# Seven planned durations of an attention and expert kernel set to other values

## Chip, cores and metric

The kernel runs on one core of a Trainium2 chip. The metric is the device time of one execution in microseconds (us). A core has TensorE (PE; its weight loads are PEld), VectorE (DVE), ScalarE (ACT), GpSimd (POOL) and SyncE (SP); here POOL and SP mainly issue DMA transfers.

## What is computed

```python
s_g = scale * np.matmul(q_g, k_all.transpose(0, 1, 3, 2))      # k_all = [k_g, k_l]
out_g = np.matmul(sm(s_g), v_all)
s_ll = np.where(abs(i - j) <= 32, scale * q_l @ k_l.T, -1e9)   # local band
s_lg = scale * np.matmul(q_l, k_g.transpose(0, 1, 3, 2))
out_l = np.matmul(sm(np.concatenate([s_lg, s_ll], axis=-1)), v_all)
x = np.concatenate([out_g, out_l], axis=2)   # 8 batches x (32 + 512) rows, 8 heads x 64
h = x @ w_in                                 # 4352 rows: 512 -> 2048
g = h * np.clip(h + 3.0, 0.0, 6.0) / 6.0
y = g @ w_out                                # 2048 -> 512
```

8 batches, 8 heads of 64, 512 local rows with a window of 32 to each side, 32 global rows; `sm` is the softmax. The attention output, 4352 rows of 512, goes through the two expert products.

## The kernel before

The kernel doesn't write its order of instructions out. It builds a list of operations (`add`), each with an engine or a choice of two (`BOTH`: ScalarE or VectorE), a planned duration in ns, the operations it depends on, a key (its rank), and the ring buffers that it takes and frees. `Plan.lay` then lays all operations in time: it keeps a time at which each engine is free, and again and again takes the operation that can start first, the lower key first among those that can start within 40 ns of each other. Of an operation with two engines it takes the one on which it would end first. A small model of the two transfer queues (`Transfers`) says when a DMA lands. What comes out is one order for each engine; each engine then runs its instructions in that order, and waits on semaphores where a producer isn't done. The planned times themselves are not in the program. `Plan.fill` puts idle matmuls (L1002) where the planned TensorE order leaves gaps before the first use of a certain accumulator, with a bound on the gap's length.

For batch b and step j (128 rows of q) a `local_step` does:
- the scores of 8 heads on TensorE: 8 matmuls against the global keys (L653) and 32 against the bands (L660) in a double accumulator `s`, of which there is one; the first two steps of batch 0 have another form (L646);
- on VectorE per head an addition of the mask with the minimum taken (L672), on ScalarE the exponential with its sum (L683);
- on VectorE per four heads a reciprocal (L693) and a multiplication into `pn` (L697);
- the turn of `pn` into `et`: up to batch 4 on TensorE (L704) with a copy back, from batch 5 on by a DMA transpose of SP (L715);
- the product with the values, `av` (L733; L725 in batch 0), in two accumulators `a`, against strips `st` of the values which SP copies together (L527) from `ve`, and the copy into `xt`, two casts by ScalarE (L295) or VectorE (L297).

For each batch, `global_steps` does the same for its 32 global rows: scores (L771, L776) that take `s` and both accumulators `a`; maxima (L784 to L788); exponentials on ScalarE (L797); sum and reciprocal (L803, L804); scaling to `pg` (L811); the turn to `eg` by TensorE (L825) or, from batch 5 on, by DMA (L819); the product with the values (L838); the copy to `xg` (L846). `place_kg` copies a batch's global keys (L619).

`moe_local` takes a batch once its attention is done: 16 groups of four matmuls with `w_in` (L860; batch 0 in two halves), each followed by a ReLU on ScalarE (L867) and a multiplication on VectorE (L871) out of one of three accumulators `m`; then 16 groups of four with `w_out` (L882), an output copy (L295, L297) and a store by SP (L897). In the order the first products of one batch stand among the attention steps of the next, and the second products after them. `moe_global` does it for all global rows at the end.

GpSimd's queue issues all loads (L411), SP's the strips, the DMA transposes (L573 for q and k from batch 4 on) and the stores.

Of the kernel before, what the change touches and what calls it, by code (L numbers as in the profile page):

```python
# [78 lines left out]
class Plan:  # L79
# [13 lines left out]
    def add(self, eng, dur, emit, deps=(), key=0.0, acq=None, rel=(), dma=None):  # L93

        o = Op(eng, dur, emit, deps, key, acq, rel, 0, dma)
        o.can = {eng: dur} if isinstance(eng, str) else dict(zip(eng, dur))
        o.n = len(self.ops)
        self.ops.append(o)
        for r in rel:
            r.held += 1  # L100
        return o
# [106 lines left out]
def kernel(  # L208
# [17 lines left out]
    S = Sg + Sl  # L226
    dm, dff = moe_w_in.shape
    NP = H // 2
    NJ = Sl // P
# [59 lines left out]
    add = plan.add  # L289
# [3 lines left out]
    def copy(op, out, in_):  # L293
        if op.eng == "ACT":
            nc.scalar.copy(out=out, in_=in_)  # L295
        else:
            nc.vector.tensor_copy(out=out, in_=in_)  # L297

    BOTH = ("ACT", "DVE")
# [103 lines left out]
    qkT, gT, kg, strip, vload = {}, {}, {}, {}, {}  # L403
# [209 lines left out]
    def place_kg(b, key, g_op=None):  # L613
        r, g = b % 2, (b // 2) % 2
        c0 = r * 2 * G + G

        def ev(op):
            for e in range(2):
                nc.vector.tensor_copy(out=kgz[r][e * D:(e + 1) * D, :, e, :],  # L619
                                      in_=gt[g][e * D:(e + 1) * D, :, c0:c0 + G])  # L620
        deps = [g_op or gT[b // 2], prep["clear"]]
        if b >= 2:
            deps += [S_op[b - 2, j] for j in range(NJ)]
        return add("DVE", 260, ev, deps, key=key)

    def local_step(b, j, key):
        r = b % 2
        kept = b == 0 and j < KEEP
# [8 lines left out]
        def pe(op):  # L637
# [17 lines left out]
            for p in range(NP):  # L655
                for u in range(NU):
                    for e in range(2):
# [2 lines left out]
                        nc.tensor.matmul(out=ps[u * UQ:(u + 1) * UQ, e, p * P + G:(p + 1) * P],  # L660
                                         lhsT=qk[r][rows, 0, p, q0:q0 + UQ],
                                         rhs=qk[r][rows, 1, p, q0 - UQ:q0 + 2 * UQ])
        s = add("PE", 1080 if kept else 960, pe, [qkT[b, j], *keyT[b, j], *(keyT[b, 0 if b == j == 0 else min(j + 1, NJ - 1)][:1] if j < NJ - 1 else ()), kg[b] if kept or b else kg0_op[0]], key=key, acq="S")
        S_op[b, j] = s
        first = None
        exs, trs = [], []
# [22 lines left out]
        for a in range(2):  # L689
# [4 lines left out]
            rec = add("DVE", 95, rc, exs[h0:h1] + [pn_op], key=key - 0.1)  # L694
# [43 lines left out]
        else:  # L738
            vs = []
            for a in range(2):  # L740
                vs.append(add("PE", 235, lambda op, a=a: av(op, a), [e_, *strip[b, j], *vs], key=key - 0.4,
                              acq=f"A{a}", rel=[et_op]))
# [4 lines left out]
        def xe(op, a):  # L747
            src = psA[a].rearrange("k (p u e q) -> k p u e q", p=2, u=NU, e=2)
            for e in range(2):
                copy(op, xt[xt_op[b].slot][e * D:(e + 1) * D, 2 * a:2 * a + 2, j * P:(j + 1) * P].rearrange(  # L750
                    "d p (u q) -> d p u q", u=NU), src[e * D:(e + 1) * D, :, :, e, :])
# [2 lines left out]
            copy(op, xt[xt_op[b].slot][:, :, j * P:(j + 1) * P], psA[0].rearrange("k (p q) -> k p q", p=NP))  # L754
        if tight:
            return [add(BOTH, (480, 610), xa, [*vs, xt_op[b]], key=key - 0.5, rel=vs)]
        return [add(BOTH, (780, 680), lambda op, a=a: xe(op, a), [v, xt_op[b]], key=key - 0.5, rel=[v])
                for a, v in enumerate(vs)]

    xt_op, xdone = {}, {}  # L760

    def global_steps(b, key):
        r, g = b % 2, (b // 2) % 2
        g0 = r * 2 * G
        deps = [gT[b // 2]] + [x for j in range(NJ) for x in keyT[b, j]]

        def pe(op):
# [5 lines left out]
            for p in range(NP):  # L773
                for e in range(2):
                    rows = slice(e * D, (e + 1) * D)
                    nc.tensor.matmul(out=psS[op.slot][p * G:(p + 1) * G, e, :], lhsT=gt[g][rows, p, g0:g0 + G],  # L776
                                     rhs=qk[r][rows, 1, p, UQ:UQ + Sl])
        s = add("PE", 750, pe, deps, key=key, acq=("S", "A0", "A1"))
        gS_op[b] = [s]
        so = add("DVE", 0, lambda op: None, [s], key=key, acq="stat")  # L780

        def red(op):
# [3 lines left out]
                nc.vector.tensor_reduce(out=w[:, 0, 2 + e:3 + e], in_=psA[e][:, 0:G], axis=AX, op=ALU.max)  # L786
            nc.vector.tensor_tensor(out=w[:, 0, 4:6], in0=w[:, 0, 0:2], in1=w[:, 0, 2:4], op=ALU.max)
            nc.vector.tensor_scalar(out=w[:, 0, 6:8], in0=w[:, 0, 4:6], scalar1=-scale, scalar2=None, op0=ALU.mult)  # L788
        rd = add("DVE", 1600, red, [so], key=key)
        xs, sgo, evs = [], [], []  # L790
        for e in range(2):
            sgo.append(add("ACT", 0, lambda op: None, [rd], key=key + 0.1 * e, acq="sg"))
# [8 lines left out]
        def rc(op):  # L801
            w = stat[so.slot]
            nc.vector.tensor_tensor(out=w[:, 1, 4:6], in0=w[:, 1, 0:2], in1=w[:, 1, 2:4], op=ALU.add)  # L803
            nc.vector.reciprocal(out=w[:, 2, 0:2], in_=w[:, 1, 4:6])  # L804
        rec = add("DVE", 150, rc, xs, key=key + 0.1)
        eg_op = None
        for e in range(2):
            po = add("DVE", 0, lambda op: None, [rec], key=key + 0.1, acq="pg")
# [32 lines left out]
        v = add("PE", 590, av, evs + [x for i in range(NV) for x in vload[b, i]], key=key, acq="A0", rel=[eg_op])  # L841
        gav[b] = v

        def xe(op):
            for e in range(2):
                nc.vector.tensor_copy(  # L846
                    out=xg[e * D:(e + 1) * D, :, b * G:(b + 1) * G],
                    in_=psA[0][e * D:(e + 1) * D, 0:256].rearrange("d (p e q) -> d p e q", p=NP, e=2)[:, :, e, :])
        return add("DVE", 400, xe, [v], key=key, rel=[v])

# [82 lines left out]
    lqk, lg, keyT, kg0_op = {}, {}, {}, []  # L935
    for b in range(B):
        if b == 0:
            seq = ["q0", "h", "q1", "k", "v0", "v1", "q2", "v2", "q3", "v3", "v4", "i0", "i1", "i2", "i3", "g"]
            for n, what in enumerate(seq):
                k, i, key = what[0], int(what[1:] or 0), -8.0 + 0.05 * n  # L940
# [38 lines left out]
        if b % 2 == 0:  # L979
            if b == 0:  # L980
                kg[0] = turn_g(0, lg[0][:1], lead - 1.5)
                gT[0] = turn_g(0, lg[0], lead + 0.5, [kg[0]])
                if KEEP < NJ:
                    kg0_op.append(place_kg(0, lead - 1.2 if KEEP == 0 else lead + 0.9, kg[0]))
            else:
                gT[b // 2] = turn_g(b, lg[b // 2], lead - 1.5)
        if b:
            kg[b] = place_kg(b, lead - 1.2)
# [7 lines left out]
        for j in range(NJ):  # L996
            xdone[b, j] = local_step(b, j, lead + j)
        xgd[b] = global_steps(b, lead + 3.6)
        moe_local(b, 4.0 * b + 0.5, 4.0)
    moe_global(4.0 * b + 2.5, 1.5)  # L1000
# [39 lines left out]
```

## Time and profile before

| | us |
|---|---|
| median of 3 runs | 345.37 |
| lowest, highest | 341.38, 347.09 |
| the profiled execution | 346.03 |
| its span, first to last instruction | 344.3 |

| engine | busy us | share of the span |
|---|---|---|
| VectorE | 271.3 | 79% |
| ScalarE | 248.7 | 72% |
| GpSimd | 105.6 | 31% |

Lines of a timeline give start and length in us, engine, source line, operation, the tile written and the tiles read, shapes and a count; in square brackets stands the idle time before and what ended it. Lines of groups give busy us in total and mean ns of one instruction. A line of busy time by stretch gives the stretch, its length, then the busy time of PE, PEld, DVE, ACT and POOL with the number of instructions, the granted TensorE clock as a share of full speed, the DMA share, and GB/s.

### The profile page before, as it was taken

To read this page: it belongs to the slowest core of one execution; us is meant where nothing else is said; L and a number is where in the kernel's file an instruction comes from. 1 tells how busy PE (TensorE), PEld (TensorE's weight loads), DVE (VectorE), ACT (ScalarE), POOL (GpSimd) and SP (SyncE) were. 2 spreads that over 40 slices of the span, in tenths; PEclk is the share of its full clock that TensorE was granted. 3 is DMA by queue.
4 is the path that set the end of the run, shared out by engine and by line. 5 is a ranking of instruction groups with operands and counts; after the bars stand their busy time and mean duration, and the time that the engine had idled before them with its cause. 6 is when DMAs were issued, how large, how long until landed. Compare 5 with 4: busy or idle time off the path is not lost.

```text
span 344.3 us, 10201 instructions
## 1 busy us (share of the span) xinstructions
PE 319.0 (93%) x3804; PEld 182.6 (53%) x3804; DVE 271.3 (79%) x1012; ACT 248.7 (72%) x834; POOL 105.6 (31%) x139
## 2 busy tenths in 40 slices
PE   7889878999979889999999999979999999999995
PEld 5768764555445445454545544444444544546642
DVE  5998898789969599969995999679977996576300
ACT  4999997549968578637995888659967997464402
POOL 8735931685377245703810310013000000000000
PEclk9999999999999999999999999999999999999999
DMA  9999999999999999999999697699953413400012
GB/s 158 195 241 163 163 187 240 159 171 190 213 122 202 224 141 159 217 231 148 190 230 194 125 181 197 152 184 155 197 123 94 71 33 91 131 1 2 30 57 98
DMA packets 158322, 52.19 MB, mean 152 GB/s; under 512 B 142656, under 2 KB 150848, under 8 KB 158272
## 3 DMA queue, kind: packets, MB, share of 16 engines
q0 software_dynamic: 106560, 17.05, 70.3%
q1 hardware_dynamic: 51712, 34.48, 45.2%
q8 instruction: 30, 0.49, 0.6%
q14 instruction: 20, 0.16, 0.2%
HBM read 35.19 MB, written 8.91 MB: 128 GB/s over the span
## 4 chain that ended last, share of the span: by engine, by line
PE 42%; DVE 24%; DMA 16%; ACT 8%; SPq 6%; issue 3%; POOL 0%; POOLq 0%; ACTq 0%; DVEq 0%
PE m L882 20%; PE m L860 14%; DMA st<-ve 8%; DVE gs L871 7%; SPq L527 5%; DVE sm L672 5%; DMA ve<-in_v_l_dram 4%; DVE pn L697 4%; ACT sm L683 3%; ACT t L867 3%; DVE xt L297 2%; PE a L733 2%; DMA sm<-in_q_l_dram 1%; ACT sg L797 1%; PE t L704 1%
## 5 line engine op out<-in xcount | busy, mean ns | idle before, releaser
L882 PE MATMUL m<-wout,gs 128*128 128x512 f16 x544 | 129.0, 379 | 1.4 <-DMA wout<-in_moe_w_out_dram 0.7
L860 PE MATMUL m<-xt,win 128*128 128x512 f16 (+1 forms) x576 | 121.6, 355 | 3.8 <-DVE gs L871 3.1
L683 ACT ACTIVATE sm<-sm,stat 128x128 f32<-128x128 f32 x256 | 100.4, 396 | 22.4 <-DVE stat L672 21.9
L871 DVE SCALAR_TENSOR_TENSOR gs<-t,m 128x512 f16<-128x512 f32 x136 | 91.2, 683 | 16.6 <-ACT t L867 15.9
L867 ACT ACTIVATE t<-m 128x512 f32<-128x512 f32 x136 | 79.8, 595 | 16.5 <-PE m L860 15.8
L860 PEld LDWEIGHTS <-win 128*128 128x128 f16 x640 | 60.0, 97 | 55.1 <-issue 7.7
L882 PEld LDWEIGHTS <-gs 128*128 128x128 f16 x544 | 49.9, 98 | 54.1 <-issue 3.7
L672 DVE CUSTOM_DVE_ANT_0 sm<-s,mask 128x128 f32<-128x128 f32 x256 | 61.0, 283 | 3.1 <-PE s L660 2.0
L683 ACT ACTIVATION_READ_ACCUMULATOR sm<-sm,stat 128x1 f32 x256 | 49.4, 193 | 0.0
L697 DVE TENSOR_TENSOR pn<-sm,stat 128x512 f16<-128x512 f32 x64 | 44.0, 688 | 0.9
L411 POOL DMA_DIRECT2D nat<-in_q_l_dram x30 | 26.8, 894 | 37.6 <-DMA qk<-nat 24.0
L295 ACT COPY ot<-m 128x512 f32<-128x512 f32 x28 | 16.4, 586 | 25.9 <-PE m L882 22.2
L411 POOL DMA_DIRECT2D ve<-in_v_l_dram x40 | 32.2, 821 | 7.7 <-PE m L860 4.8
L411 POOL DMA_DIRECT2D nat<-in_k_l_dram x30 | 26.7, 892 | 12.8 <-DMA nat<-in_k_l_dram 4.9
L295 ACT CAST xt<-a 64x256 f16<-64x256 f32 (+1 forms) x63 | 23.7, 376 | 9.6 <-PE a L733 9.1
L733 PEld LDWEIGHTS <-st 128*128 128x128 f16 x448 | 20.1, 98 | 15.3 <-issue 4.8
L733 PE MATMUL a<-et,st 128*128 128x64 f16 x448 | 22.7, 193 | 4.1 <-DMA st<-ve 4.0
L297 DVE CAST xt<-a 64x256 f16<-64x256 f32 (+1 forms) x53 | 22.6, 426 | 4.8 <-PE a L733 3.6
L411 POOL DMA_DIRECT2D ve<-in_v_g_dram x8 | 4.8, 596 | 53.4 <-PE a L838 53.3
L672 DVE DVE_READ_ACCUMULATOR2_ANT stat<- 128x1 f32 x256 | 21.0, 82 | 0.0
L704 PE MATMUL t<-ident,pn 128*128 128x128 f16 x160 | 13.4, 220 | 1.6 <-DVE pn L697 1.6
L693 DVE RECIPROCAL stat<-stat 128x4 f32<-128x4 f32 x64 | 11.1, 173 | 3.8 <-ACT sm L683 3.4
(88 smaller groups left out, 262.4 us busy)
## 6 DMA issues: line engine op xcount, KB each, us to landing
out_dram<-ot SPq DMA_DIRECT2D x32, 256.0 KB, 3.0
st<-ve SPq DMA_DIRECT2D x14, 384.0 KB, 7.7
nat<-in_q_l_dram POOLq DMA_DIRECT2D x30, 128.0 KB, 8.7
nat<-in_k_l_dram POOLq DMA_DIRECT2D x30, 128.0 KB, 8.5
st<-ve SPq DMA_DIRECT2D x7, 512.0 KB, 8.1
st<-ve SPq DMA_DIRECT2D x14, 256.0 KB, 8.7
ve<-in_v_l_dram POOLq DMA_DIRECT2D x24, 128.0 KB, 6.4
st<-ve SPq DMA_DIRECT2D x18, 128.0 KB, 7.1
```

Of the source, the lines that this page charges most:

```text
L295: nc.scalar.copy(out=out, in_=in_)
L297: nc.vector.tensor_copy(out=out, in_=in_)
L411: nc.gpsimd.dma_start(out=dst(op), in_=src)
L527: nc.sync.dma_start(out=dst, in_=src)
L672: nc.vector.tensor_tensor_reduce(out=sm[sm_op.slot][:, h, :], in0=psS[s.slot][:, e, p * P:(p + 1) * P], in1=m, scale=-scale, scalar=3.0e38 ...
L683: nc.scalar.activation(out=sm[sm_op.slot][:, h, :], in_=sm[sm_op.slot][:, h, :], func=EXP, scale=-1.0, bias=stat[stat_op.slot][:, 0, h:h + 1],
L697: (nc.gpsimd if op.eng == "POOL" else nc.vector).tensor_tensor(out=pn[pn_op.slot][:, h0:h1, :], in0=sm[sm_op.slot][:, h0:h1, :], in1=stat[ ...
L733: nc.tensor.matmul(out=psA[a][:, c0:c0 + 64], lhsT=st[r][:, u * NJ + j, p * P:(p + 1) * P], rhs=et[et_op.slot][:, 2 * p:2 * p + 2, u * UQ: ...
L860: nc.tensor.matmul(out=psM[op.slot][:, i * n:(i + 1) * n], lhsT=w_in_t[:, m, (c + i) * P:(c + i + 1) * P], rhs=x()[:, m, t0:t0 + n], start ...
L867: nc.scalar.activation(out=t1[to.slot], in_=psM[f.slot], func=RELU, bias=0.5, scale=1.0 / 6.0)
L871: nc.vector.scalar_tensor_tensor(out=gs[set_.slot][:, c:c + k, t0:t0 + n], in0=t1[to.slot].rearrange("f (k t) -> f k t", k=k), scalar=1.0, ...
L882: nc.tensor.matmul(out=psM[(f or op).slot], lhsT=gs[set_.slot][:, c, t0:t0 + P], rhs=w_out_t[:, c, :], start=(c == 0), stop=(c == NDFF - 1))
```

## The change

Seven planned durations take other values: the scores and the global scores on TensorE, and on VectorE the placing of the global keys, the copy into `xt` (in the pair, ScalarE's value too), the global maxima, the global sum and reciprocal, and the copy to `xg`. No operation, dependency, key or buffer is edited; all five orders are laid anew from the new numbers, and with them the choice of engine of operations that have one.

```diff
@@ place_kg
-        return add("DVE", 260, ev, deps, key=key)
+        return add("DVE", 390, ev, deps, key=key)
@@ local_step
-        s = add("PE", 1080 if kept else 960, pe, [qkT[b, j], ...
+        s = add("PE", 900 if kept else 600, pe, [qkT[b, j], ...
...
-        return [add(BOTH, (780, 680), lambda op, a=a: xe(op, a), [v, xt_op[b]], key=key - 0.5, rel=[v])
+        return [add(BOTH, (750, 870), lambda op, a=a: xe(op, a), [v, xt_op[b]], key=key - 0.5, rel=[v])
@@ global_steps
-        s = add("PE", 750, pe, deps, key=key, acq=("S", "A0", "A1"))
+        s = add("PE", 400, pe, deps, key=key, acq=("S", "A0", "A1"))
...
-        rd = add("DVE", 1600, red, [so], key=key)
+        rd = add("DVE", 1800, red, [so], key=key)
...
-        rec = add("DVE", 150, rc, xs, key=key + 0.1)
+        rec = add("DVE", 400, rc, xs, key=key + 0.1)
...
-        return add("DVE", 400, xe, [v], key=key, rel=[v])
+        return add("DVE", 580, xe, [v], key=key, rel=[v])
```

In the two programs TensorE has the same work apart from the idle matmuls, of which 24 stand in the new order and 19 in the old (each runs as two instructions). Of the operations with a choice of engine, 26 go from VectorE to ScalarE and 25 the other way.

More of the change, by code (lines that the diff above doesn't have):

```diff
@@ L662, in pe @@
                                          rhs=qk[r][rows, 1, p, q0 - UQ:q0 + 2 * UQ])
-        s = add("PE", 1080 if kept else 960, pe, [qkT[b, j], *keyT[b, j], *(keyT[b, 0 if b == j == 0 else min(j + 1, NJ - 1)][:1] if j < NJ - 1 else ()), kg[b] if kept or b else kg0_op[0]], key=key, acq="S")
+        s = add("PE", 900 if kept else 600, pe, [qkT[b, j], *keyT[b, j], *(keyT[b, 0 if b == j == 0 else min(j + 1, NJ - 1)][:1] if j < NJ - 1 else ()), kg[b] if kept or b else kg0_op[0]], key=key, acq="S")
         S_op[b, j] = s
```

## Prediction

> **What bounds the kernel now.** I read the page's first part, then the waits of TensorE, then busy time by stretch, then the timeline at the waits found.
>
> ```profile
> PE 319.0 (93%) x3804; PEld 182.6 (53%) x3804; DVE 271.3 (79%) x1012; ACT 248.7 (72%) x834; POOL 105.6 (31%) x139
> ```
>
> TensorE's queue runs in program order and is busy 93% of 344.3 us, so the time is its work plus its waits. The change edits only numbers that the planner uses; its instructions stay the same but for idle fill. Only the waits can move, and these are the ones to know:
>
> ```profile
> PE a L733 <- DMA st<-ve: 4.0, 3, 2.5
> PE m L860 <- DVE gs L871: 3.1, 7, 0.7
> PE a L838 <- DMA eg<-pg: 2.1, 1, 2.1
> PE s L653 <- DVE stat L672: 2.0, 3, 1.1
> PE t L704 <- DVE pn L697: 1.6, 4, 0.8
> ```
>
> Columns: total us, times, longest us. Two kinds stand here: a transfer that lands later than the order supposed (st, eg), and VectorE work that comes late (gs, stat, pn). The second kind belongs to the stretches in which a batch's first expert product (L860) runs beside attention:
>
> ```profile
> 118.00:139.00 21.00, 18.34 (x259) 10.57 (x260) 18.50 (x65) 16.28 (x51) 9.81 (x12) 1.00 1.92 160
> 195.00:212.00 17.00, 16.75 (x142) 8.07 (x140) 16.56 (x58) 15.40 (x51) 4.36 (x6) 1.00 1.16 184
> 231.00:249.00 18.00, 16.65 (x194) 8.32 (x197) 17.62 (x61) 15.26 (x52) 4.57 (x6) 1.00 1.46 183
> 299.00:337.00 38.00, 38.00 (x227) 20.64 (x225) 17.09 (x26) 16.71 (x29) 0.00 (x0) 1.00 0.08 29
> ```
>
> After each stretch's length come PE, PEld, DVE and ACT busy. From 195 to 212 and from 231 to 249 VectorE has 0.4 us free of 17 or 18: it paces there. From 299 on TensorE alone works, without a wait; on TensorE the new order is the old one from the last L860 group of batch 6 (near 281 us) to the end, so nothing is to be had there.
>
> **The change, part by part.** First, are the new numbers nearer to the chip?
>
> ```profile
> 128.13 0.35 PE L653 MATMUL s<-kgz,qk 128*128 128x32 f16 x8
> 128.42 0.36 PE L660 MATMUL s<-qk 64*32 64x96 f16 x32
> 128.74 0.59 PE L860 MATMUL m<-xt,win 128*128 128x512 f16 x2
> ```
>
> A score block holds TensorE from 128.13 to 128.74, 0.61 us. The plan had 960 ns and now has 600. With 30 such blocks the old plan had 30 x 0.35 = 10.5 us of TensorE time that the chip does not spend; the chip used it to catch up after waits that the plan had not foreseen.
>
> ```profile
> L295 ACT CAST xt<-a 64x256 f16<-64x256 f32 x60 | 21.9, 366 | 9.6 <-PE a L733 9.1
> L297 DVE CAST xt<-a 64x256 f16<-64x256 f32 x52 | 21.9, 421 | 4.8 <-PE a L733 3.6 <-ACT xt L295 0.6
> ```
>
> The copy of an attention output is two such casts: 2 x 421 = 842 ns on VectorE (plan 680, now 870), 2 x 366 = 732 on ScalarE (780, now 750). So more of these go to ScalarE: 13 ops change to it and 11 away. These numbers are better; whether the order is better must be read at the waits.
>
> Now the program order, old against new. SP's queue is unchanged for its first 43 transfers, GpSimd's for its first 62 loads. TensorE's differs by single attention blocks that pass up to nine expert groups (a group: four matmuls of L860 or L882), forward or back.
>
> *The front, to 55 us.* Five more idle fills (L1002) stand in TensorE's queue, ten instructions.
>
> ```profile
> 1.19 3.38 PE L1002 MATMUL a<-idle 128*128 128x256 f32 x8 [1.19 <-DVE idle L379]
> ```
> ```profile
> 9.59 3.19 PE L1002 MATMUL a<-idle 128*128 128x256 f32 x14
> ```
>
> At 3.19/14 = 0.23 us each they are 2.3 us. What hides them is a transfer:
>
> ```profile
> 55.10 1.89 PE L882 MATMUL m<-wout,gs 128*128 128x512 f16 x8 [0.73 <-DMA wout<-in_moe_w_out_dram]
> ```
>
> At 55.1 TensorE stands for w_out, whose load is issued at the same place in both programs. I take 0; bounds 0, since the landing excludes a gain, and +1.6 (2.3 less the 0.73 of idle), which the next wait would swallow.
>
> *The wait of batch 2.* The first attention-times-value block (av) of batch 2 waits for its strips:
>
> ```profile
> 93.10 1.03 PE L882 MATMUL m<-wout,gs 128*128 128x512 f16 x4
> 93.97 0.25 PE L733 MATMUL a<-et,st 128*128 128x64 f16 x3
> 96.71 0.31 PE L733 MATMUL a<-et,st 128*128 128x64 f16 x5 [2.49 <-DMA st<-ve]
> ```
>
> The strips land in the same order behind the same loads, so the resumption stays near 96.7. The new order has one block more ahead of it, the score block of step 3: 0.6 us of the 2.49 is used. Gain 0.6; bounds 0 (TensorE arrives up to 1.9 us later than now) and 0.6. What would be late next is again these strips.
>
> *The wait of batch 3.*
>
> ```profile
> 117.22 0.25 PE L733 MATMUL a<-et,st 128*128 128x64 f16 x3
> 118.77 0.31 PE L733 MATMUL a<-et,st 128*128 128x64 f16 x5 [1.30 <-DMA st<-ve]
> 118.92 0.44 PE L825 MATMUL t<-ident,pg 128*128 128x128 f16 x5
> ```
>
> Between the two avs the old queue takes from 96.71 to 117.22, 20.5 us. The new one puts 3.3 us more there: two L860 groups at 0.87 (93.10 to 93.97 is one group), a score block (0.61), an av of the global rows (its row, below, has 0.74; 0.6 to the next start) and 18 transposes (five in 0.44, so at most 1.6; taken 1.0) come in, 3.9, and the block of step 3 (0.61) has gone in front. It reaches the second av at 96.7 + 20.5 + 3.3 = 120.5, 1.8 us behind the strips' landing at 118.7. So the 1.30 us goes entirely; GpSimd also issues batch 3's six v loads ahead of two q and k loads of batch 4, which can only bring the strips sooner. Gain 1.3; bounds 0 (were the strips 3.1 us later) and 1.3.
>
> *The stretch from 118 to 139.* PE's row above has 2.66 us of idle in it, 1.30 of them the wait just counted; VectorE has 2.5 idle of 21. Two copies that stand in VectorE's queue here leave it, the one of the global rows to before 118, the one of qk to ScalarE:
>
> ```profile
> 125.31 0.59 DVE L846 CAST xg<-a 64x128 f16<-64x128 f32 x2
> 125.93 0.69 DVE L297 COPY qk<-t 128x1024 f16<-128x1024 f16 x1
> ```
>
> L871 follows 1.28 us sooner if VectorE paces all of it. I take 1.0, bounds 0 and 1.3.
>
> *Stretches 195 to 212 and 231 to 249.* Here the new order is not kind. In VectorE's queue, counted from a batch's first L871 to its last, the score reductions rise from 8 to 18 in the first and from 9 to 14 in the second; they used to stand in the following L882 stretch. In the chain of waits one is
>
> ```profile
> 224.03 0.20 DVE sm L672
> ```
>
> so 10 x 0.20 = 2.0 us and 5 x 0.20 = 1.0 us more where VectorE paces. In each, one xt copy (0.84) leaves for ScalarE; the first gains one pn and the second loses one (0.69, row below), and the first gains an output copy of about that length: +2.5 and -0.5. In the first, TensorE also gets two L882 groups and two score blocks, 2 x 0.87 + 2 x 0.61 = 3.0 us, so the stretch grows, but by work that is not lost. I take +0.3 net, bounds -0.5 and +2.5.
>
> *The wait of batch 5's global rows.*
>
> ```profile
> 220.40 1.31 SPq L573 DMA_TRANSPOSE qk<-nat  x1
> 221.80 0.53 SPq L897 DMA_DIRECT2D out_dram<-ot  x1
> 222.39 2.78 SPq L573 DMA_TRANSPOSE qk<-nat  x2
> 225.26 3.44 SPq L819 DMA_TRANSPOSE eg<-pg  x2
> ```
>
> SP's queue: the two eg transposes stand behind three qk transposes (an et transpose and a store are ahead of these); for them waits
>
> ```profile
> 230.24 0.74 PE L838 MATMUL a<-eg,ve 128*128 128x64 f16 x20 [2.06 <-DMA eg<-pg]
> ```
>
> The feeding chain on VectorE, and ScalarE's copy in the middle of it:
>
> ```profile
> 217.48 0.18 DVE L693 RECIPROCAL stat<-stat 128x4 f32<-128x4 f32 x1 [0.54 <-ACT sm L683]
> 217.69 0.69 DVE L697 TENSOR_TENSOR pn<-sm,stat 128x512 f16<-128x512 f32 x1
> 218.30 1.22 DVE L784 TENSOR_REDUCE stat<-s 128x2 f32<-128x1024 f32 x1
> ...
> 223.11 0.91 DVE L811 TENSOR_SCALAR pg<-sg,stat 128x544 f16<-128x544 f32 x2
> ```
> ```profile
> 221.15 0.58 ACT L295 COPY ot<-m 128x512 f32<-128x512 f32 x1
> ```
>
> New: the global maxima (L784) stand before that reciprocal and pn (0.8 us sooner), and ScalarE no longer copies an output between the two exponentials (0.5 of its 0.58 is in the chain). On SP one output store (0.53 and a gap of 0.1) leaves the queue ahead of eg, and two qk transposes go before the et transpose instead of waiting behind it. So pg is ready near 222.8 and eg can start near 223.8 instead of 225.26. The distance in TensorE's queue from the global scores to this av is the same. Gain 1.5; bounds 0 and 2.06. The price: that et transpose goes up to 2.6 us later (two qk transposes at 1.31), ahead of the avs of step 3; I take it as hidden by the expert groups in front of them, and as part of the bound 0 if not.
>
> Sum against the profiled execution (346.03 us, span 344.3 and 1.7 around it): -0.6 - 1.3 - 1.0 + 0.3 - 1.5 = -4.1, so 341.9. The median shown is 345.37, 0.7 below that execution; I keep 341.9, a gain of 1.0% on the median.
>
> **The rivals.**
>
> *Slower: scores brought forward choke VectorE.* Three score blocks (step 2 and 3 of batch 5, step 3 of batch 6) stand 4, 4 and 7 expert groups earlier. If the whole VectorE tail of each, 8 x 0.20 for reductions and 2 x 0.69 for pn, 3.0 us, falls where VectorE has 0.4 us free and pushes L871, TensorE's three accumulators fill and it stands: 3 x 3.0 = 9.0. It decides once more than about 0.4 us of it lies before the batch's last L871. With the two gains on the strips (1.9) kept and the others given up, 346.0 + 9.0 - 1.9 = 353.1. For: the counts 8 to 18 and 9 to 14. Against: only the reductions move over, and TensorE's own work moves along. 0.14.
>
> *No net change: waits only move.* Strips and L871 are late by the chip's pace, not by the order; what is saved at 118 is lost by 180. VectorE's 18.50 of 21 speaks for it, the solid tail against. About 345.5. 0.20.
>
> *A bigger gain.* With VectorE costed rightly, the waits on gs, stat and pn (3.1 + 2.0 + 1.6 = 6.7) shrink as well by some three quarters, 5: 337. For: TensorE resumes the moment VectorE is done in many of these, so any earlier placing counts. Against: VectorE has no more room than before. 0.16.
>
> *A slow TensorE after a long wait.* The first eight fill instructions take 3.38 us, 0.42 each, against the later 0.23: the trace's front shows TensorE at half pace. If a new wait were longer than the longest one now (2.49, after which it goes on at once at full pace), such a front could recur: 3.4 us at half pace costs 1.7 and the wait itself some 2 more than now: 346.0 - 4.1 + 3.7 = 345.6. 0.03. [...]
>
> **How the numbers follow.** The forecast, 339 to 344, has what is left: 0.47. Range 336.5 to 351: down to the bigger gain, up through the unchanged case to short of the slow rival; outside are that rival's upper part and a gain beyond 337, 0.2 together. A measurement of this kernel tells about 2% from no change: 338.5 and 352.3 around 345.37. Faster 0.17 (the bigger gain and a sliver of the forecast), slower 0.13 (most of the slow rival), within 0.70.
>
> **What would show it.** Right: the longest wait on st falls to about 1.9 us and only one of the two late ones is left; the wait on eg falls to about 0.6; PE idle within the batch 2 stretch falls by about 1; the last 38 us are unchanged; PE's busy count is ten higher on L1002. Wrong: the wait on gs L871 rises over 5 us in total (slow rival), or falls under 1 (bigger gain), or strips land later than 97 and 119 for a reason in the queues.

## Result, and the profile after

| us | before | after |
|---|---|---|
| median (20 runs each) | 344.17 | 342.49 |
| lowest | 341.38 | 336.38 |
| the profiled execution | 346.03 | 343.87 |
| its span | 344.3 | 342.1 |

The ratio of the new kernel to the old is 0.9873, 95% interval 0.9838 to 0.9908. It leaves out the runs over 1.5% above each kernel's quickest, and so keeps 8 of the new kernel's 20 (one of those left out took 407.74), while the plain medians give 342.49 / 344.17 = 0.995. The gain is thus somewhere from 0.5 to 1.3%. The forecast was 341.9. The sum of the terms was nearly right. The terms were not.

The first part of the page after, and the chain that ended last, by engine (before it was PE 42%, DVE 24%, DMA 16%, ACT 8%, SP's queue 6%):

```profile
PE 321.8 (94%) x3814; PEld 186.5 (55%) x3814; DVE 268.8 (79%) x1009; ACT 251.3 (73%) x837; POOL 105.7 (31%) x139
...
PE 57%; DVE 21%; ACT 9%; DMA 8%; SPq 2%; issue 2%; ACTq 0%; DVEq 0%
```

The waits of TensorE after (total us, times, longest us):

```profile
PE a L733 <- DMA et<-pn: 5.2, 1, 5.2
...
PE m L860 <- DVE gs L871: 1.8, 5, 0.6
...
PE a L838 <- DMA eg<-pg: 0.6, 1, 0.6
```

The waits for strips have gone, the wait on eg fell from 2.1 to 0.6, the waits on gs from 3.1 to 1.8. At the top stands one that the first trace of the kernel before doesn't have: 5.2 us, once, for an attention transpose (et). The stretches that the prediction showed, after:

```profile
118.00:139.00 21.00, 20.66 (x225) 10.97 (x224) 20.64 (x78) 19.42 (x67) 11.96 (x16) 1.00 1.94 167
195.00:212.00 17.00, 11.76 (x113) 5.97 (x112) 10.07 (x33) 10.29 (x34) 0.00 (x0) 0.90 1.05 198
231.00:249.00 18.00, 17.30 (x183) 8.67 (x181) 17.35 (x62) 17.15 (x60) 1.42 (x2) 1.00 1.20 194
299.00:337.00 38.00, 38.00 (x209) 20.35 (x208) 15.89 (x24) 16.23 (x28) 0.00 (x0) 1.00 0.09 31
```

From 118 to 139 TensorE was busy 18.34 us and is now busy 20.66. From 195 to 212 it was busy 16.75 us and is now busy 11.76, at a granted clock of 0.90. The first stretch gains; the second gives it back.

How much, the two queues tell. For single expert groups I added the usual durations of all that stands ahead in TensorE's queue (0.865 us for a group of four matmuls, 0.58 for a score block, and so on), and took that from the group's start on the chip: what is left is how late TensorE is. Lateness before less lateness after is the lead of the new kernel, worked out here from both traces and both queues:

```
expert group             before at   after at   lead of after
batch 0, w_out, first        50.68      53.12      -2.4
batch 1, w_out, first        93.10      93.16      -0.1
batch 1, w_out, 9th         106.75      99.54      +2.7
batch 2, w_in, 9th          128.74     123.44      +5.5
batch 2, w_out, 9th         147.83     141.24      +6.6
batch 3, w_out, first       176.86     170.21      +6.7
batch 4, w_in, first        195.30     186.33      +6.7
batch 4, w_in, 9th          203.43     203.37      +0.1
batch 4, w_out, 9th         219.41     219.94      +0.3
batch 5, w_in, first        231.40     229.79      +1.6
batch 5, w_out, first       249.23     246.72      +2.5
batch 6, w_out, 9th         290.36     288.22      +2.2
```

The expert groups of a batch run beside the attention of the next. The new kernel is 6.7 us ahead until 190 us, loses all of it between 190 and 203, and gains 2 us again at the end. In the timeline of TensorE after, this is the place:

```profile
200.84 0.59 PE L733 MATMUL a<-et,st 128*128 128x64 f16 x8 [5.24 <-DMA et<-pn]
201.23 1.90 PE L860 MATMUL m<-xt,win 128*128 128x512 f16 x4
```

The block is the first attention-times-values product (av) of batch 5, step 0. The group of four matmuls of L860 behind the wait takes 1.90 us, where the prediction's rows have 1.03 for four. The chain of waits of the same kernel shows what the block waited for (start, us, what):

```profile
179.71 4.43 SPq L573
...
184.24 5.67 DMA out_dram<-ot
...
189.99 0.69 DVE ot L297
...
191.14 9.65 DMA et<-pn
...
200.84 0.59 PE a L733 x8
```

From 179.71 to 200.84 nothing in this chain is TensorE's: SP's queue, a store, an output copy that needs the store's buffer, some score reductions of VectorE (not shown), and then the transpose, 9.65 us from its issue to its landing. That VectorE released the transpose is inferred by the profile, and the rows of the two engines say otherwise. VectorE's last row for the transpose's input ends at 188.06, and SP, without a pause since 178.14, issued the transpose at 191.14 (VectorE's timeline, then SP's):

```profile
187.37 0.69 DVE L697 TENSOR_TENSOR pn<-sm,stat 128x512 f16<-128x512 f32 x1
```
```profile
178.14 6.00 SPq L573 DMA_TRANSPOSE qk<-nat  x2
...
184.83 2.07 SPq L573 DMA_TRANSPOSE qk<-nat  x1
186.99 1.13 SPq L897 DMA_DIRECT2D out_dram<-ot  x1
188.22 1.90 SPq L573 DMA_TRANSPOSE qk<-nat  x1
190.22 0.83 SPq L897 DMA_DIRECT2D out_dram<-ot  x1
191.14 2.01 SPq L715 DMA_TRANSPOSE et<-pn  x1
```

In the kernel before, the input was written at 195.28 and the transpose issued at 195.30:

```profile
194.59 0.69 DVE L697 TENSOR_TENSOR pn<-sm,stat 128x512 f16<-128x512 f32 x1
```
```profile
184.29 4.03 SPq L573 DMA_TRANSPOSE qk<-nat  x3
...
189.01 1.30 SPq L573 DMA_TRANSPOSE qk<-nat  x1
192.26 0.33 SPq L897 DMA_DIRECT2D out_dram<-ot  x1
195.30 1.23 SPq L715 DMA_TRANSPOSE et<-pn  x1
```

In both orders the four qk transposes of batch 6 and the same stores stand ahead of this transpose in SP's queue. Before, they were done by the time the input was. Now the input comes 7.2 us sooner, they are not done, and the transpose stands behind them for 3.1 us. It is not that SP began late: the first of the four is issued at 178.14 and no longer at 184.29, 6.2 us sooner. But SP is through with these items only 1.5 us sooner, at 191.05 for 192.59: the issues of the four took 9.97 us for 5.33, and they landed 6.2 to 9.5 us after their issue, where it had been 3.1 to 4.6.

The other half is the transfer: it landed 9.65 us after its issue, and 5.3 us in the kernel before. Among what else was in flight were batch 6's six value loads. GpSimd now issues them from 185.81 on, ahead of the transpose; in the kernel before it began with them at 194.79, half a microsecond ahead of it. The first of the six, after:

```profile
185.81 0.58 POOL L411 DMA_DIRECT2D ve<-in_v_g_dram  x1 [11.74 <-PE a L838]
```

But transfers were slow before these loads began: the second qk transpose took 4.43 us to issue, until 184.1, and the loads of q and k that GpSimd issued from 160 to 173 us landed 11.6 to 15.6 us after their issue, and 5.5 to 7.4 in the kernel before. Why is not shown.

Theory: the lead is lost since SP's queue and the transfers were not done as much sooner as TensorE was. Rivals: the value loads alone slow the transpose; the half pace of TensorE behind the wait costs part of it; the wait is an accident of one execution; or the VectorE stretch chokes, as in the prediction's slow rival, and the wait only hides it.

### The profile page after: what moved, and what is told of

Same layout as the page of the kernel before. It is cut to its first block, busy times and chain, and to the rows that moved or that the text cites. A ratio compares the mean times of both kernels' runs of the same rounds, so it can differ in the third digit from the quotient of the medians.

```text
span 342.1 us, 10211 instructions
## 1 busy us (share of the span) xinstructions
PE 321.8 (94%) x3814; PEld 186.5 (55%) x3814; DVE 268.8 (79%) x1009; ACT 251.3 (73%) x837; POOL 105.7 (31%) x139
## 4 chain that ended last, share of the span: by engine, by line
PE 57%; DVE 21%; ACT 9%; DMA 8%; SPq 2%; issue 2%; ACTq 0%; DVEq 0%
PE m L882 28%; PE m L860 18%; DVE gs L871 7%; DVE sm L672 4%; ACT sm L683 3%; ACT t L867 3%; DMA et<-pn 3%; DVE pn L697 3%; PE a L733 2%; DMA out_dram<-ot 2%; PE t L704 2%; DVE xt L297 2%; DMA sm<-in_q_l_dram 1%; PE a L838 1%; PE s L660 1%
## 5 line engine op out<-in xcount | busy, mean ns | idle before, releaser
L860 PE MATMUL m<-xt,win 128*128 128x512 f16 (+1 forms) x576 | 124.2, 361 | 3.3 <-DVE gs L871 1.8
L860 PEld LDWEIGHTS <-win 128*128 128x128 f16 x640 | 60.4, 99 | 53.3 <-issue 6.3
L411 POOL DMA_DIRECT2D nat<-in_q_l_dram x30 | 27.1, 904 | 24.5 <-DMA nat<-in_q_l_dram 10.8
L295 ACT CAST xt<-a 64x256 f16<-64x256 f32 (+1 forms) x67 | 25.1, 375 | 12.1 <-PE a L733 11.5
L733 PEld LDWEIGHTS <-st 128*128 128x128 f16 x448 | 20.5, 99 | 16.8 <-issue 6.1
L295 ACT COPY ot<-m 128x512 f32<-128x512 f32 x24 | 14.0, 586 | 21.1 <-PE m L882 14.9
L733 PE MATMUL a<-et,st 128*128 128x64 f16 x448 | 22.7, 195 | 5.2 <-DMA et<-pn 5.2
L297 DVE CAST xt<-a 64x256 f16<-64x256 f32 (+1 forms) x49 | 20.9, 426 | 3.6 <-PE a L733 2.9
L1002 PE MATMUL a<-idle 128*128 128x256 f32 x48 | 14.3, 436 | 1.2 <-DVE idle L379 1.2
## 6 DMA issues: line engine op xcount, KB each, us to landing
nat<-in_q_l_dram POOLq DMA_DIRECT2D x30, 128.0 KB, 11.6
```

Of the source, the lines that this page charges most:

```text
L411: nc.gpsimd.dma_start(out=dst(op), in_=src)
L733: nc.tensor.matmul(out=psA[a][:, c0:c0 + 64], lhsT=st[r][:, u * NJ + j, p * P:(p + 1) * P], rhs=et[et_op.slot][:, 2 * p:2 * p + 2, u * UQ: ...
L860: nc.tensor.matmul(out=psM[op.slot][:, i * n:(i + 1) * n], lhsT=w_in_t[:, m, (c + i) * P:(c + i + 1) * P], rhs=x()[:, m, t0:t0 + n], start ...
L1002: order = plan.fill(plan.lay(), lambda: nc.tensor.matmul(out=psA[1][:, 0:256], lhsT=idle.bitcast(FP32)[:, 0:P], rhs=idle.bitcast(FP32)), "A1")
```

## The experiments

Each ratio is to the kernel before on the same chip beside it (its medians there: 343.25 for the first four, 343.68 for the next four, 343.52 for the last four). Some kernels move operations of the finished order with a small function, `behind(order, moved, target)`: it puts the operations `moved`, named by their numbers in the plan, right behind `target`, and what depends on them after them.

**The new kernel again** (`after_again`), unchanged.

> The changed kernel once more. Theory of the collision: TensorE is some 6 us ahead of the old kernel near 190 us, and loses it at the first av of batch 5, which waits for the DMA transpose of et; the wait is again the longest of TensorE, 3 to 6 us, and the granted clock falls below 1 behind it; time 338 to 344. Theory of the pace: the gain up to 190 us was a chance of one execution; then TensorE is less than 3 us ahead there this time, and the wait on et is short.

Median 341.31 of 12 runs, 0.993 of before (0.9899 to 0.9962). The wait is there again:

```profile
201.51 0.58 PE L733 MATMUL a<-et,st 128*128 128x64 f16 x8 [5.71 <-DMA et<-pn]
```

So is the lead: it is 6.7 us at the first w_out group of batch 3 and gone at the ninth w_in group of batch 4. So neither is the accident of one execution. But the two profiled executions, 343.87 and 344.84 (the slowest of the 12), are not among the quick ones of this kernel, which go down to 336.38; how long the wait is in those is not shown.

**The av later in TensorE's queue** (`av_later`).

The two avs of batch 5, step 0, go behind a later `w_in` group (the 13th of batch 4):

```diff
-    order = plan.fill(plan.lay(), lambda: nc.tensor.matmul(
+    laid = plan.lay()
+    byn = {o.n: o for o in laid}
+    laid = behind(laid, [byn[n] for n in (1438, 1439)], byn[1343])
+    order = plan.fill(laid, lambda: nc.tensor.matmul(
```

> The changed kernel with the two av blocks of batch 5 step 0 (and what hangs on them) put behind six expert groups more, c7 to c12 of batch 4; nothing else is moved. Theory of the collision: the wait on et falls under 1 us, the granted clock stays 1.0, and the time falls by 4 to 7 us against the changed kernel, to 335 to 338. Theory of the pace: the groups brought forward wait for VectorE or the next transfer instead, the wait returns at the av of step 1 or at the strips of batch 6, and the time is within 1.5 us of the changed kernel.

Six runs between 337.62 and 345.39, median 344.0; the ratio, 0.9864 (0.9813 to 0.9916), rests on two of them. No steady gain, and not the 335 to 338 of my theory. TensorE's waits at L733:

```profile
PE a L733 <- DMA st<-ve: 3.1, 2, 2.9
PE a L733 <- DMA et<-pn: 2.3, 1, 2.3
```

The wait did not go; it went over to the next transpose and to strips, which are the next things on SP's queue. The lead is still there at the ninth w_in group of batch 4 and gone at the ninth w_out group. So more than one block meets a late transfer.

**TensorE kept busy in the wait** (`warm`).

```diff
+        def keep_warm(n):
+            for _ in range(n):
+                nc.tensor.matmul(out=psT[0].bitcast(FP32)[:, 0:256], lhsT=idle.bitcast(FP32)[:, 0:P], rhs=idle.bitcast(FP32))
...
+            if (b, j, a) == (5, 0, 0):
+                keep_warm(8)
```

> The changed kernel with eight idle matmul pairs (3.4 us) put into the wait, just ahead of the first av of batch 5. If the half clock behind the wait costs time: the granted clock stays 1.0 and the time falls by 1 to 2 us against the changed kernel, the wait on et itself shortened to 2 us with the end of it unchanged. If the clock behind the wait costs nothing: within 0.5 us. If the wait is short in most executions: up to 3 us slower.

Busy time by stretch, first of the new kernel (`after_again`), then of this one; the column after the five engines is the granted clock:

```profile
190.00:212.00 22.00, 15.94 (x167) 7.91 (x165) 13.74 (x47) 14.13 (x48) 0.34 (x1) 0.84 1.30 185
```
```profile
190.00:212.00 22.00, 20.43 (x210) 11.35 (x209) 16.58 (x59) 16.11 (x57) 0.00 (x0) 1.00 1.30 183
```

The clock goes from 0.84 to 1.00 over this stretch, and the median is 342.12 beside 341.31: nothing gained. The half pace is real (the four matmuls of L860 behind the first av take 1.90 us in `after_again` and 1.03 here), and filling the wait saves nothing that the medians show. A reason may be that TensorE next stands for the second transpose (0.81 us at 202.54 in this trace); that it is the reason is not shown.

**Without batch 6's value loads** (`no_v6`). Leaves out the six loads of batch 6's values, so batch 6 is computed with the values that lie in that buffer, batch 4's.

```diff
-    def load(dst, src, packets, key, deps=(), acq=None, ns=ROW, desc=None):
+    def load(dst, src, packets, key, deps=(), acq=None, ns=ROW, desc=None, skip=False):
...
-            nc.gpsimd.dma_start(out=dst(op), in_=src)
+            if not skip:
+                nc.gpsimd.dma_start(out=dst(op), in_=src)
...
-                      key + 0.001, deps))
+                      key + 0.001, deps, skip=b == 6))
```

> The changed kernel without the loads of the values of batch 6, so that batch 6 is computed with the values of batch 4. These six loads are issued near 186 to 190 us, just ahead of the et transpose. Collision with these loads: the transpose lands within 4.5 us of the end of its issue instead of 7.6, the wait on et falls to 2 us or less, the time to 336 to 339. Collision with the strips, the stores or the transposes of q and k instead: the landing takes 7 us or more and the wait stays 4 us or more.

335.75 us in one run, beside 343.25. The long wait is gone and TensorE is all but solid:

```profile
190.00:212.00 22.00, 21.60 (x217) 10.49 (x216) 19.95 (x70) 19.64 (x70) 0.00 (x0) 1.00 0.89 170
```

The DMA share falls from 1.30 to 0.89, and the transpose lands 4.5 us after its issue. This takes the slow rival away: VectorE, busy 19.95 of 22, does not hold TensorE once the transfer is there. What the loads have to do with it, this one run does not show. Its first two qk transposes, issued at 179 and 181 us, where the loads have not begun in `after` either, landed in 4.3 and 5.3 us and not in 8.7 and 9.5, so its transfers were quicker beforehand; and the changed kernel, with its loads, has a run of 336.38. The next two tell more.

**The value loads later** (`held`).

Batch 4's global av, for whose end the value loads of batch 6 wait, goes behind the second av of batch 5, step 1:

```diff
+    laid = behind(laid, [byn[1292]], byn[1469])
```

> The changed kernel, complete, with one block of TensorE moved: the global av of batch 4 (L838), which frees the tile that batch 6's values go into, stands behind the second av of batch 5 step 1 instead of 14 groups before; so batch 6's six value loads are issued some 15 us later, after the two et transposes. Theory of the collision with these loads: the first et transpose lands within 5 us of its issue, the wait on et falls from 5.5 to 1 us or less, the granted clock is 1.0, the time 336 to 339. Rival, that the transposes of q and k, the stores and the strips are enough to hold et up: a wait of 3 us or more stays and the time stays at 340 or more. Possible loss: batch 6's strips come later, and its first av waits.

Median 348.09, 1.0113 of before (1.0073 to 1.0153): slower.

SP's and GpSimd's timelines, and TensorE's with the av of step 0 and a later one:

```profile
189.46 2.11 SPq L715 DMA_TRANSPOSE et<-pn  x1
```
```profile
204.94 0.59 POOL L411 DMA_DIRECT2D ve<-in_v_g_dram  x1 [34.37 <-PE a L838]
```
```profile
196.91 0.44 PE L733 MATMUL a<-et,st 128*128 128x64 f16 x8 [2.25 <-DMA et<-pn]
223.89 0.61 PE L733 MATMUL a<-et,st 128*128 128x64 f16 x8 [5.49 <-DMA et<-pn]
```

The first wait shrinks from 5.24 to 2.25 and doesn't go: with the first value load issued at 204.94, the transpose of 189.46 still took 7.4 us to land. So a slow landing does not need these loads; the qk transposes of this run, 8.3 to 11.8 us, are as slow as in `after`. A new wait of 5.49 comes 27 us later, since the loads feed batch 6's strips, and the seven strips now stand in SP's queue ahead of a later transpose:

```profile
207.77 11.66 SPq L527 DMA_DIRECT2D st<-ve  x7
219.53 1.55 SPq L715 DMA_TRANSPOSE et<-pn  x1
```

**The transpose ahead on SP's queue** (`et_first`). The loads stay where they are; the qk transposes of batch 6, steps 2 and 3, go behind the et transpose of batch 5, step 1:

```diff
+    laid = behind(laid, [byn[n] for n in (1669, 1670)], byn[1467])
```

> The changed kernel with the transposes of q and k of batch 6, steps 2 and 3, moved on SP's queue from ahead of the two et transposes of batch 5 to behind them; the value loads stay where they are. Theory of the collision with the loads: et is issued 3 us sooner but still takes 7 us to land; the wait falls to 2 to 4 us, the time by 1.5 to 3 us to 338.5 to 340. Rival, SP's own queue is what holds et up: the wait vanishes, time 336 to 338.

Median 338.62, 0.9836 of before (0.978 to 0.9892). SP's queue, and TensorE's timeline:

```profile
185.54 1.26 SPq L715 DMA_TRANSPOSE et<-pn  x1
...
193.62 4.59 SPq L573 DMA_TRANSPOSE qk<-nat  x2
```
```profile
192.95 0.41 PE L733 MATMUL a<-et,st 128*128 128x64 f16 x8
```

The transpose is issued at 185.54, right behind its input (written at 185.52), and the av begins at 192.95, without a wait in front. It still takes 7.4 us to land, as it did in `held` without the value loads beside it; it is only issued early enough now. What is left is 1.1 us at the next transpose. The lead, worked out as in the table, stays: 9 us ahead of this place and 9 behind it. So half of each expectation came: the slow landing of the one, the vanished wait of the other. The order of SP's queue is the cause that can be mended, and this one move takes 2.7 us off `after_again`'s 341.31 (ratios 0.9836 and 0.993, whose intervals lie apart; that of the first comparison, 0.9873, overlaps with this one). The profiled execution, 335.64, is the quickest of the six.

**Only the TensorE numbers** (`pe_only`) **and only the VectorE numbers** (`dve_only`).

Both against the kernel before; `pe_only` is

```diff
-        s = add("PE", 1080 if kept else 960, pe, [qkT[b, j], ...
+        s = add("PE", 900 if kept else 600, pe, [qkT[b, j], ...
...
-        s = add("PE", 750, pe, deps, key=key, acq=("S", "A0", "A1"))
+        s = add("PE", 400, pe, deps, key=key, acq=("S", "A0", "A1"))
```

and `dve_only` has the other five lines of the change's diff.

> The kernel before with the two TensorE durations alone changed (scores, global scores). If the gain up to 190 us comes of the TensorE durations, which are most of what the plan had wrong (13 us of TensorE time): lead of 4 us or more over the kernel before at batch 4's second products, time 337 to 343. If it comes of the VectorE numbers: no lead, 343 to 347.

> The kernel before with the five VectorE durations (and ScalarE's in the pair) alone changed. If these make the gain: a lead of 4 us or more at batch 4's second products, time 337 to 343. If the TensorE durations make it: no lead, 343 to 348, since VectorE's stretches are planned longer and TensorE's blocks stay too long.

The TensorE numbers alone: 338.0, 0.9808 (0.976 to 0.9857). The VectorE numbers alone: 343.78, 0.9992 (0.9962 to 1.0021). The five VectorE durations are worth nothing by themselves; together with the others they seem to cost some 3 us (341.31 or 342.49 against 338.0; of the ratios, 0.993 lies clear of 0.9808, and the interval of 0.9873 overlaps with it). The first of TensorE's waits in `dve_only`:

```profile
PE m L860 <- DVE gs L871: 5.0, 11, 1.3
```

gs rose from 3.1 to 5.0, in one trace each, with numbers that are nearer to the chip. The leads over the first trace of the kernel before, at batch 4's ninth w_out group, are 7.4 us for `pe_only` and 2.6 for `dve_only`.

**The kernel before, a second time** (`before_again`), one run.

> The kernel before, profiled a second time, unchanged. Question: are its two waits for strips (2.49 us at 96.71, 1.30 us at 118.77), which the prediction took as pinned to 96.7 and 118.7, a property of the order? If yes: waits on the strips of 3 to 4.5 us in total again, near 96.5 and 118.5. If the landing time scatters from one execution to the next (five later kernels with the same queues landed batch 2's last strip between 91 and 96.5): less than 2 us in total, and the profiled execution nearer to 341 than to 346.

345.98, and other waits. All those of TensorE's timeline for a transfer of st, et or eg:

```profile
27.96 0.59 PE L725 MATMUL a<-et,st 128*64 128x32 f16 x26 [1.58 <-DMA st<-ve]
96.92 0.30 PE L733 MATMUL a<-et,st 128*128 128x64 f16 x5 [1.02 <-DMA st<-ve]
199.98 0.44 PE L733 MATMUL a<-et,st 128*128 128x64 f16 x8 [1.39 <-DMA et<-pn]
229.62 0.81 PE L838 MATMUL a<-eg,ve 128*128 128x64 f16 x20 [2.08 <-DMA eg<-pg]
```

The wait on eg comes back (2.06 and 2.08). The waits for strips, 2.6 us in total, lie between my two cases: 1.02 in place of 2.49 at 97, none at 118, and one of 1.58 at 28 that was not there. At 97 the landing is the same, 96.8 us after 96.6 for batch 2's last strip, and the wait is shorter since TensorE came 1.7 us later. At 118 the landing moved: batch 3's last strip came at 115.3 and not at 118.6. The wait on et, 1.39 us, is new: also the kernel before can meet this transpose too soon, where it takes 6.8 us to land and not 5.3. The time is that of the first profile; what one place lost another took.

**Each TensorE number alone** (`sc_only`: 1080/960 to 900/600; `gs_only`: 750 to 400).

> The kernel before with the durations of the local scores alone (1080/960 to 900/600). 30 blocks carry 0.36 us each of plan time that the chip doesn't spend, against 16 global blocks of 0.35. If the gain of the two TensorE numbers together (338.0, 0.981 of before) belongs to the local scores: 0.980 to 0.987 of before, 337 to 340. If the global scores carry it: 0.995 to 1.002. If they add up: about 0.987 to 0.99.

> The kernel before with the duration of the global scores alone (750 to 400). If the local scores carry the gain: 0.995 to 1.002 of before. If the two add up by their plan time (5.6 us of 16.4): about 0.993. If the global scores carry it: 0.980 to 0.987.

(There are 8 global score blocks and not the 16 of the expectation, so 2.8 us of plan time stand beside 10.8.) `sc_only`: 338.41, 0.985 (0.9802 to 0.9898), as the two together. `gs_only`: 348.4, 1.0133 (1.0092 to 1.0174), slower, which none of my three cases had: a corrected number that costs 4.9 us. Its timeline of SP and of TensorE:

```profile
206.23 1.50 SPq L715 DMA_TRANSPOSE et<-pn  x1
207.82 6.31 SPq L573 DMA_TRANSPOSE qk<-nat  x4
214.23 1.29 SPq L715 DMA_TRANSPOSE et<-pn  x1
```
```profile
218.95 0.41 PE L733 MATMUL a<-et,st 128*128 128x64 f16 x8 [3.12 <-DMA et<-pn]
```

The same mechanism in another place: an attention transpose behind four qk transposes, 6.31 us, and a wait of 3.12 for it. Its input was written at 212.63, so about half of the wait is the queue and the rest the landing, 4.7 us where the kernel before has 3.1. The lead over the kernel before, 4.6 us at 195, is gone at 219. In the kernel before, the two attention transposes stand next to each other there, ahead of the qk ones. This profiled execution is the quickest of the six, 346.55, and its trace loses the lead and no more; what makes the median 4.9 us slower is not shown.

**TensorE numbers and the transpose ahead** (`pe_et`), the attempt to beat all.

The move of `et_first`, made in `pe_only`:

```diff
+    laid = behind(laid, [byn[n] for n in (1669, 1670)], byn[1467])
```

> The two TensorE durations alone, and on SP the two qk transposes of batch 6, steps 2 and 3, behind the attention transpose of batch 5, step 1, as in the order et_first. With the TensorE durations alone that attention transpose was only just in time (0.3 us of wait), so if the wait on it is all that this move can save, 0.978 to 0.982 of before, no better than the two durations alone. If the earlier transpose also lets batch 5's blocks run ahead in TensorE's queue later on: 0.970 to 0.977. If the moved qk transposes come too late for batch 6: above 0.985.

338.04, 0.9846 (0.9806 to 0.9885). Nothing beyond `pe_only`: there the transpose was in time already. `pe_only`, `sc_only`, `et_first` and `pe_et` lie within 0.6 us and can't be told apart; all four are 1.5 to 1.9% below the kernel before. Their medians are also below the changed kernel's, but the interval of its first ratio, 0.9873, overlaps with theirs.

## Why the prediction was right, and where it was not

The time was foreseen within 0.6 us of the median and the range held it. On the profiled executions 4.1 us were foreseen and 2.2 came (346.03 to 343.87), and that by luck, out of two larger errors: the gains up to 190 us were 6.7 and not 2.9, and a loss of 6.6 behind it was not foreseen at all. Against `before_again`, worked out in the same way, the lead before 190 us is 4.5 us; so some 2 us of the 6.7 are the scatter of the kernel before.

*The front: as foreseen.* With five more idle fills the kernel is 2.4 us behind at 53 us (their price had been worked out as 2.3), and at 93 it is level.

*Strips of batches 2 and 3: batch 2's mis-sized, batch 3's as foreseen.* For batch 2, 0.6 was foreseen, and the whole wait went: the lead goes from -0.1 at 93 to +2.7 at 100. The step "the strips land in the same order behind the same loads, so the resumption stays near 96.7" failed: batch 2's last strip landed at 91.2 in the first trace of after, and between 91.1 and 96.4 in the seven profiles whose order is the same up to there. In the two profiles of the kernel before it landed at 96.6 and 96.8. Whether the new order brings it sooner or these two lie at the late end of a scatter is open. The 1.3 of batch 3 came, but the wait was one of a single execution: `before_again` doesn't have it. A wait seen in one execution should have been given a range that includes its not being there.

*The stretch from 118 to 139: its size is not known.* Foreseen 1.0 with an upper bound of 1.3; against the first trace the lead grew by 2.9 there (2.7 to 5.5), of which 1.3 is the wait of batch 3's strips, and by another 1.1 to 147. Against `before_again` it grew by only 0.4 over the same groups. The row that the prediction read, VectorE with 2.5 us of idle time, was one execution's: `before_again`, in the old order, has VectorE busy 20.65 of 21 us, and the new kernel 20.64. So the rival "a bigger gain" may have a share in it or not; which of the numbers made what gain there is open (TensorE is busy 20.05 us of this stretch in `sc_only` and 20.14 in `gs_only`).

*Stretches 195 to 212 and 231 to 249: the step that failed.* I asked only whether VectorE would choke there (+0.3, bound +2.5). It did not: VectorE is busy 10.07 of 17 us. TensorE stood instead for a transfer, 5.24 us and about 1.4 us more behind it, 6.6 in all. The term was not in the sum. The prediction has a transpose of batch 5 that moves behind two qk transposes, and says "I take it as hidden by the expert groups in front of them". That is step 3's. Step 0's did not change its place in the queue, so it has no term; but its input came 7.2 us sooner, and what stood ahead of it in SP's queue, begun 6.2 us sooner, was done only 1.5 us sooner. The distance in the queue was the same and the time was not. My bound for a late transpose was "the bound 0" of another term, a gain not made, where `gs_only` and `after` show a loss of 3 to 7 us.

*The wait on eg: right.* Foreseen a gain of 1.5 and a wait of about 0.6; the wait is 0.6, and the lead grows by 1.3 from 220 to 230. The kernel before has this wait in both of its profiles.

*The last 38 us: unchanged*, as foreseen, 38.00 busy of 38.

*The rivals.* "Scores brought forward choke VectorE" is refuted by `no_v6`: with the same order on the three compute engines and the transfers out of the way, TensorE is busy 21.60 of 22 us. "A slow TensorE after a long wait" came true in its first half: a wait longer than any before (5.24 us), and half pace behind it (granted clock 0.50 from 200.84 to 204, four matmuls in 1.90 us for 1.03). That this is the slow front of the trace come again was my estimate; no run shows what makes the front slow. The price of 1.7 us that this rival put on it is not seen in the median of `warm`. "No net change" describes the path of the lead well, 6.7 to 0.1, by another mechanism than the one it named.

What stays open: why the transfers land so slowly from 160 us on, and what part the six value loads have in it (`held` has 7.4 us without them beside the transpose, `no_v6` 4.5 in one run); and which of the five VectorE numbers turns the order that `pe_only` has into one in which TensorE meets the transpose 5 us too soon.

## What to carry to other kernels

When a change moves one engine ahead, go through every queue that feeds it and ask what sets each transfer's issue: its input, which moves along, or what stands ahead of it in its queue, which may start sooner and still not be done as much sooner (here 6.2 us and 1.5); an unchanged place in a queue is no reason to skip it. Better numbers in a planner give a different order, and not always a better one: here one corrected number was worth 1.5%, one cost 1.3%, and five did nothing. A wait from a single trace, and the idle time of a stretch, need a second trace before they are treated as fixed, and so does a cause that one run seems to show.

## What the hardware showed

Waits of nearly one length had different granted clocks behind them. The wait on eg of the kernel before, in two executions, by stretch around its end (first trace, then `before_again`):

```profile
229.00:231.00 2.00, 0.76 (x28) 0.79 (x28) 0.00 (x0) 0.64 (x3) 0.00 (x0) 1.00 0.84 215
231.00:233.00 2.00, 2.00 (x47) 1.06 (x44) 1.85 (x7) 0.07 (x1) 1.81 (x3) 1.00 0.94 231
```
```profile
229.00:231.00 2.00, 1.38 (x60) 1.25 (x60) 0.51 (x2) 0.01 (x1) 0.45 (x1) 0.79 0.92 228
231.00:233.00 2.00, 2.00 (x19) 0.74 (x6) 1.90 (x12) 0.54 (x3) 1.97 (x4) 0.50 0.95 197
```

After 2.06 us of waiting TensorE went on at full clock, 1.00; after 2.08 us it had 0.79 and 0.50. The prediction took 2.49 us as safe from one trace, which has 1.00 behind that wait, from 96.71 to 99; after 5.24 us it was 0.66 in `after`, from 200 to 205. So a wait of some 2 us was followed by half pace in one of two executions of the same kernel, and its length did not tell which.

The second surprise is how far a DMA transpose's landing moves. All twelve of the et transposes of the kernel after, from issue (their minimum, median and maximum):

```profile
DMA to landing us min/median/max: 3.0/3.1/9.7
```

Half of them take 3.1 us or less; the two issued at 191 and 195 us took 9.65 and 9.3, and 10.5 and 11.4 in `after_again`.
